# A fused attention and expert kernel: the first eleven stretches in another written order, and 1 / deviation of tiles 2 and 3 by GpSimd's power operation too

## The chip, the cores and the metric

The kernel runs on one core of a Trainium2 chip. The metric is device time in microseconds (us), the median of three runs. Five engines work side by side, each in the order of its own instruction list: TensorE (PE in the profile, its weight loads PEld), VectorE (DVE), ScalarE (ACT), GpSimd (POOL) and SyncE (SP), which here only issues transfers. ACT can issue transfers on a queue of its own.

## The reference

The input `x` is 2048 tokens of 640 values in bf16. It is normalized; the attention has 32 heads of 192 and, for all tokens, the last 512 keys and values of a cache. Its output is gated by an expert block that changes two tokens only.

```python
xn = _layernorm(x, axis=-1)                      # (x - mean) / sqrt(var + 1e-5)
q = (xn @ wq) -> heads;  k, v = last 512 rows of each head's cache
p = softmax(q @ k^T * 192 ** -0.5);  s = (p @ v) -> rows @ wo
r = xn @ w_r; the two tokens with the largest r get y = (silu(x_sel w_gate) * (x_sel w_up)) w_down * sigmoid(r)
g = silu(xn, with y added at those two tokens)
return x + s * g
```

## The kernel before

**Tiling.** The tokens are 16 tiles of 128 (n = 0 to 15), in four blocks of four tiles (t5). Heads are taken in pairs; two pairs make a group (g). A step i is one block with one pair: `steps[i]` is (g, t5, pr) with the pair innermost, so steps 0 and 1 are block 0 with pairs 0 and 1, steps 2 and 3 block 1, and so on to 8 steps for a group. A step has four units, one for each token tile, so unit n belongs to step n // 4. Units are worked in stretches: S.0 has units 0 and 1, S.1 units 2 and 3, S.2 units 4 to 6, then three in each stretch; 86 stretches in all. One stretch computes scores, row maxima, exponentials and their transposes for its units, and beside them the q projection of later steps (`q`), the product with v for the units of the stretch before (`O`) and the output projection (`W`).

**Order.** Nothing is scheduled by a planner: `manual_schedule` keeps every engine to the order in which the program calls it. For the first eleven stretches (S.0 to S.10) and what comes ahead of them this order is the token list `FIRST`, written out by hand; from S.11 on the function `stretch(j)` makes it, and a list `LAST` closes the kernel. Each token calls one function through `first(token)`. All engines read the same list; a token adds to the engine it names, so moving it past a token of another engine changes nothing, and moving it past one of the same engine, or the same queue, does.

**The tokens.** `x.t.lo.hi` loads token tiles of block t; `k.p.h`, `v.p`, `wq.p` load keys, values and q weights of pair p, `wo.g.pr` half of a group's output weights (SyncE's queue; with `.a`, ACT's). `kT.p` transposes the keys by DMA, `kt.q.e` half of pair 0's on TensorE. `bn.n.c` is one half of tile n's statistics on VectorE, the second half with the aggregate; `as.n` is both on ACT, in two passes. `sq` and `rc` make 1 / deviation by ACT's square root and VectorE's reciprocal; `pw.lo.hi` makes it on GpSimd, in four small operations of which the second is a power (line 212). `sx` and `ex` load ACT's tables for the square root and the exponential. `ap.n.e` applies the normalization, `turn.n.e` transposes a tile on TensorE with the copy on the engine named, `xT.lo.hi` transposes tiles by DMA. `q.i.c` is one third of step i's q (five matmuls; with `.lo.hi` for half a block), `qe.i.c.e` its eviction: the engine letter counts only without the trailing `.lo.hi`, with it ACT does it. `S.j` are the scores of a stretch in two passes (lines 315 and 322), `M` a row maximum (VectorE), `E` an exponential (ACT), `P.n` the DMA transpose of a unit's probabilities, `R` the reciprocal of the sums, `O.n` and `OO.n.m` the products with v, `Oe.n.e` their eviction, `T.j` the DMA transpose of a stretch's outputs, `W.w` the output projection of a token tile for one group, `We.w.e` its eviction. `B.j.s` runs background work of the expert block; for j up to 10 there is none, so these tokens do nothing.

**What holds an instruction back.** TensorE writes into eight banks: two of tag f (q, the transposes, single `O`) and six of tag p (scores, `OO`, `W`). A bank comes free with the eviction of what it held. SyncE issues its transfers one after the other, and each of eight semaphores is taken again only when the transfer before on it has landed. The block buffer of `x` has two slots, so block 2's load waits until block 0 has been applied.

Of the kernel before, what the change touches and what calls it, by code (L numbers as in the profile page):

```python
# [21 lines left out]
def kernel(ctx, tc, A_x, A_k_cache, A_v_cache, A_wq, A_wo, B_x, B_w_r, B_w_gate, B_w_up, B_w_down, out):  # L22
    nc = tc.nc
    P = 128
    _, S, D = A_x.shape
# [754 lines left out]
    for j in range(2, NST):  # L780
        due = sum(st_of[4 * i] <= j + 1 for i, _ in todo)
        k = max(due, 2) if j % 4 != 1 else max(due, 3)
# [3 lines left out]
        k = 2 if len(ready) >= 2 and len(q_in[j]) <= 2 and (done + 1) <= 1.5 * (j - 4) else 1  # L786
        k = {NST - 4: 1, NST - 3: 1, NST - 2: 3, NST - 1: 2}.get(j, k)
# [69 lines left out]

    for token in FIRST:
# [43 lines left out]
```

## Time and profile before

| | us |
|---|---|
| median of 3 runs | 809.0 |
| the runs | 807.45, 809.0, 809.56 |
| the profiled execution | 808.71 |
| its span | 806.9 |
| TensorE busy in the span | 785.0 (97%) |
| VectorE, ACT, GpSimd busy | 623.1, 480.5, 171.9 |

The span is what the profile covers; the rest of the execution's time lies around it. TensorE's busy time counts a matmul from its issue to a modelled end. In the views that follow, a timeline row gives the start in us, the duration, the engine, the source line, the operation, output and inputs, and in brackets how long the engine had been idle and what ended that. "SPq" is SyncE issuing a transfer; its duration is that of the issue. A row of transfers gives output and input, the number of issues, the size and the median time from issue to landing.

### The profile page before, as it was taken

To read this page: it belongs to the slowest core of one execution; us is meant where nothing else is said; L and a number is where in the kernel's file an instruction comes from. 1 tells how busy PE (TensorE), PEld (TensorE's weight loads), DVE (VectorE), ACT (ScalarE), POOL (GpSimd) and SP (SyncE) were. 2 spreads that over 40 slices of the span, in tenths; PEclk is the share of its full clock that TensorE was granted. 3 is DMA by queue.
4 is the path that set the end of the run, shared out by engine and by line. 5 is a ranking of instruction groups with operands and counts; after the bars stand their busy time and mean duration, and the time that the engine had idled before them with its cause. 6 is when DMAs were issued, how large, how long until landed. Compare 5 with 4: busy or idle time off the path is not lost. (4 is left out here: it accounts for less than half of the span.)

```text
span 806.9 us, 15632 instructions
## 1 busy us (share of the span) xinstructions
PE 785.0 (97%) x5748; PEld 481.6 (60%) x5748; DVE 623.1 (77%) x1242; ACT 480.5 (60%) x1299; POOL 171.9 (21%) x187
## 2 busy tenths in 40 slices
PE   7799999999999999999999999999999999999996
PEld 3355555666566665666656665666665666566665
DVE  6775478989887777777777777777788888777786
ACT  5796666565556655665555565566556865565560
POOL 0330000000000000000001899920000000265954
PEclk9999999999999999999999999999999999999999
DMA  8999898799979999799997899869997899997994
GB/s 224 201 209 219 159 208 134 134 187 183 187 124 206 198 210 210 128 209 213 188 229 145 163 180 202 160 122 184 201 166 134 148 180 209 167 194 153 167 177 117
DMA packets 453389, 143.80 MB, mean 178 GB/s; under 512 B 422350, under 2 KB 452816, under 8 KB 453312
## 3 DMA queue, kind: packets, MB, share of 16 engines
q1 hardware_dynamic: 451712, 139.94, 93.3%
q0 software_dynamic: 928, 2.50, 1.1%
q8 instruction: 45, 0.74, 0.4%
q10 hardware_dynamic: 672, 0.36, 0.1%
q14 instruction: 32, 0.26, 0.1%
HBM read 39.98 MB, written 2.62 MB: 53 GB/s over the span
## 5 line engine op out<-in xcount | busy, mean ns | idle before, releaser
L337 ACT ACTIVATE pexp<-sc,nm 128x512 bf16<-128x512 f32 x512 | 348.0, 695 | 287.4 <-issue 241.8
L330 DVE TENSOR_REDUCE nm<-sc 128x1 f32<-128x512 f32 x512 | 315.0, 681 | 74.8 <-PE sc L322 74.8
L301 PE MATMUL q_ps<-xnT,wq_p 128*128 128x512 bf16 (+1 forms) x975 | 227.4, 379 | 7.5 <-DMA xnT<-xn 2.6
L404 PE MATMUL w_ps<-wo_g,oT 128*128 128x320 bf16 x1542 | 223.6, 299 | 0.8 <-DMA wo_g<-in_A_wo_dram 0.6
L404 PEld LDWEIGHTS <-oT 128*128 128x128 bf16 x1542 | 150.1, 98 | 72.0 <-issue 1.5
L356 PE MATMUL o_ps<-v_sb,pT 128*128 128x192 bf16 x2048 | 185.2, 246 | 4.4 <-DMA pT<-pexp 4.4
L356 PEld LDWEIGHTS <-pT 128*128 128x128 bf16 x2048 | 171.1, 98 | 18.2 <-DMA pT<-pexp 5.3
L371 DVE TENSOR_TENSOR o_sb<-o_ps,lsum 128x384 bf16<-128x384 f32 x245 | 134.9, 556 | 49.2 <-PE o_ps L356 31.0
L301 PEld LDWEIGHTS <-wq_p 128*128 128x128 bf16 x975 | 89.0, 98 | 132.8 <-issue 41.3
L315 PE MATMUL sc<-kT,qT 128*128 128x512 bf16 x512 | 125.4, 379 | 0.5 <-DVE o_sb L371 0.3
L418 DVE TENSOR_TENSOR s_acc<-s_acc,w_ps 128x320 f32<-128x320 f32 x192 | 92.1, 483 | 32.1 <-PE w_ps L404 32.1
L337 ACT ACTIVATION_READ_ACCUMULATOR pexp<-sc,nm 128x1 f32 x512 | 109.6, 214 | 0.0
L293 ACT ACTIVATE qT<-q_ps 128x512 bf16<-128x512 f32 (+1 forms) x184 | 101.5, 605 | 3.4 <-PE q_ps L301 3.2
L315 PEld LDWEIGHTS <-qT 128*128 128x128 bf16 x512 | 48.9, 98 | 41.7 <-issue 0.7
L322 PE MATMUL sc<-kT,qT 64*128 64x512 bf16 x512 | 70.3, 380 | 0.0
L643 POOL TENSOR_TENSOR s_acc<-s_acc,xn 128x640 f32<-128x640 f32 x16 | 22.4, 1401 | 114.1 <-DVE s_acc L418 114.1
L322 PEld LDWEIGHTS <-qT 64*128 64x128 bf16 x512 | 18.0, 94 | 47.0 <-issue 36.2
L622 POOL TENSOR_TENSOR xn<-xn,yh 128x640 bf16<-128x640 bf16 x32 | 44.6, 1393 | 2.7
L612 POOL DMA_DIRECT2D y_d<-y_sb x4 | 2.2, 551 | 172.5 <-DVE y_sb L609 172.5
L644 POOL TENSOR_TENSOR s_acc<-s_acc,x_fin 128x640 f32<-128x640 f32 x16 | 22.4, 1398 | 62.8 <-DMA x_fin<-in_A_x_dram 61.9
L489 POOL DMA_DIRECT2D c_d<-cand x1 | 0.6, 551 | 158.6 <-DVE cand L487 158.6
L621 POOL TENSOR_SCALAR yh<-y_bc,oh 128x640 bf16<-128x640 bf16 x32 | 25.6, 798 | 4.5 <-DMA y_bc<-y_d 2.9
(104 smaller groups left out, 222.8 us busy)
## 6 DMA issues: line engine op xcount, KB each, us to landing
wq_p<-in_A_wq_dram SPq DMA_DIRECT2D x16, 480.0 KB, 5.3
wo_g<-in_A_wo_dram SPq DMA_DIRECT2D x16, 480.0 KB, 4.5
v_sb<-in_A_v_cache_dram SPq DMA_DIRECT2D x16, 384.0 KB, 3.9
k_raw<-in_A_k_cache_dram SPq DMA_DIRECT2D x31, 192.0 KB, 3.3
pT<-pexp SPq DMA_TRANSPOSE x256, 3.7
x_fin<-in_A_x_dram SPq DMA_DIRECT2D x16, 160.0 KB, 2.8
x_in<-in_A_x_dram SPq DMA_DIRECT2D x6, 320.0 KB, 4.1
wgu<-in_B_w_gate_dram SPq DMA_DIRECT2D x15, 128.0 KB, 2.6
```

The source lines that it names most:

```text
L293: nc.scalar.activation(out=out, in_=in_, func=ACT.Copy, scale=scale)
L301: nc.tensor.matmul(q_ps, lhsT=wq_of[g * PAIRS + pr][:, dc, c * P:(c + 1) * P], rhs=xnT[:, t5 * 4 + lo:t5 * 4 + hi, dc, :], start=(dc == 0) ...
L315: nc.tensor.matmul(sc_of[n][hh], lhsT=qT_of[i][:, 2 * hh, u * P:(u + 1) * P], rhs=kp[:, :, 2 * hh, :], start=True, stop=False)
L322: nc.tensor.matmul(sc_of[n][hh], lhsT=qT_of[i][hs, 1, u * P:(u + 1) * P], rhs=kp[hs, :, 1, :], start=False, stop=True)
L330: nc.vector.tensor_reduce(out=nm_of[j][:, c:c + 1], in_=sc_of[n][hh], axis=AX.X, op=ALU.max, negate=True)
L337: nc.scalar.activation(out=pe_of[n][:, hh, :], in_=sc_of[n][hh], func=ACT.Exp, bias=nm_of[j][:, c:c + 1], scale=1.0, accum_out=l_of[j][:, ...
L356: nc.tensor.matmul(ps[:, hh, :], lhsT=pT_of[n][:, hh, jj, :], rhs=v_sb[:, hh, jj, :], start=(jj == 0), stop=(jj == NJ - 1))
L371: nc.vector.tensor_tensor(out=osb_of[j][:, m], in0=ps, in1=l_of[j][:, 2 * m:2 * m + 2].unsqueeze(2).to_broadcast([P, 2, Dh]), op=ALU.mult)
L404: nc.tensor.matmul(w_ps, lhsT=oT_of[j][:, stretches[j].index(n), c % 3, :], rhs=wo_of[g][:, c, lo:hi], start=(c == 0), stop=(c == CPG - 1))
L418: nc.vector.tensor_tensor(out=acc, in0=acc, in1=w_ps, op=ALU.add)
L621: nc.gpsimd.tensor_scalar(out=yh, in0=M["y_bc"][:, j, :], scalar1=M["oh"][:, n, j:j + 1], scalar2=0.0, op0=ALU.mult, op1=ALU.add)
L622: nc.gpsimd.tensor_tensor(out=xn[:, n, :], in0=xn[:, n, :], in1=yh, op=ALU.add)
```

## The change

The tokens of the prologue and of S.0 to S.10 are put into another order, and some change their engine. Ahead of S.0, tile 0 is now loaded from ACT's queue and tile 2 from SyncE's; wq.0 goes ahead of tile 3; half of pair 0's keys, half of pair 1's and wq.1 are issued by ACT. The second half of pair 0's keys and the copy of tile 1 are taken from the transposing bank by VectorE, that of tile 0 by ACT. `sq.2.4` and `rc.2.4` are replaced by `pw.2.4`. The exponential's table is loaded ahead of the first q evictions. In the first eleven stretches the statistics of tiles 4, 8, 12 and 15 go from VectorE to ACT, and those of 9 and 13 from ACT to VectorE. `kT.1` moves from S.0 to S.1, behind the loads of block 2 and `v.0`; `v.1` goes ahead of `v.0`. `P.1` moves from S.0 to S.1, behind them too; `turn.2`'s copy goes from ACT to VectorE. O.0 moves from S.2 to S.1. In S.6 to S.8, `P.15` goes between the two transposes of tiles 12 to 15; `v.2` goes from S.6 to S.7, `wq.2` from SyncE in S.6 to ACT in S.7, `k.3.0` from S.8 to S.7; `P.19`, `P.20` and `P.21` stand together in S.8, ahead of `k.3.1` and `wq.3`. The matmuls are the same; W.4, W.5 and others change their place by a few tokens. From S.11 on nothing is changed. Seven lines of each side of the diff follow: the prologue, S.0 to S.2 and S.6 to S.8.

```diff
-x.0.2.3.a x.0.0.1 x.0.1.2 bn.0.0 bn.1.0 bn.0.1 bn.1.1 sq.0.1 sq.1.2 rc.0.1 k.0.0 rc.1.2 k.0.1 ap.0.v ap.1.v x.0.3.4 sx wq.0 kt.0.a x.1.0.2 kt.1.a turn.0.v turn.1.a x.1.2.4 q.0.0.0.2 q.0.2.0.2 B.2.0 bn.2.0 qe.0.0.v.0.2 q.0.1.0.2 qe.0.2.v.0.2 bn.3.0 qe.0.1.v.0.2 bn.2.1 wq.1 bn.3.1 sq.2.4 bn.7.0 ex rc.2.4 ap.3.v k.1.0 ap.2.v
- S.0 turn.3.a M.0.1 M.0.0 turn.2.a E.0.0 q.0.0.2.4 bn.7.1 q.0.2.2.4 k.1.1 M.1.0 qe.0.0.v.2.4 M.1.1 E.1.0 v.0 q.0.1.2.4 bn.6.0 kT.1 bn.6.1 qe.0.2.a.2.4 qe.0.1.v.2.4 as.5 bn.4.0 x.2.0.2 v.1 bn.4.1 E.1.1 E.0.1 P.1
- S.1 M.2.0 E.2.0 M.2.1 q.1.2 x.2.2.4 pw.4.8 E.2.1 qe.1.2.a bn.8.0 bn.8.1 P.2 q.1.0 M.3.0 M.3.1 qe.1.0.a ap.7.g ap.5.v q.1.1 B.3.3 ap.4.v E.3.0 ap.6.v E.3.1 P.0 xT.4.6 qe.1.1.a
- S.2 R.0 M.4.0 M.5.0 bn.11.0 O.1 as.9 O.0 M.4.1 bn.11.1 E.4.0 as.10 xT.6.8 M.5.1 M.6.0 pw.8.12 Oe.0.a E.4.1 E.5.0 Oe.1.a E.6.0 R.1 P.3 q.2.0 M.6.1 qe.2.0.v q.2.1 x.3.2.4 q.2.2 B.4.0 B.2.1 qe.2.1.v B.2.3 P.4 ap.11.v T.0 E.6.1 P.6 O.2 E.5.1 qe.2.2.v
...
- S.6 Oe.12.a M.17.0 ap.13.g xT.14.16 q.5.2 xT.12.14 M.16.0 M.18.0 M.17.1 v.2 E.17.0 P.15 B.8.0 E.16.0 qe.5.2.v M.16.1 wo.1.0 E.18.0 E.16.1 R.5 B.7.0 k.2.0.a B.5.2 W.2 M.18.1 E.18.1 q.6.0 E.17.1 B.8.3 B.5.0 qe.6.0.a B.4.2 k.2.1 W.1 We.1.v OO.13.14 Oe.13.v We.2.a wq.2 Oe.14.v P.16 O.15
- S.7 M.19.0 P.17 M.20.0 M.21.0 Oe.15.a E.19.0 M.19.1 M.21.1 B.6.0 T.4 q.6.1 P.18 R.6 E.20.0 T.5 M.20.1 qe.6.1.a q.6.2 E.19.1 W.3 E.20.1 qe.6.2.v E.21.0 OO.16.17 Oe.16.a E.21.1 We.3.a O.18 Oe.17.v W.4 P.19 We.4.a P.21
- S.8 Oe.18.v B.9.1 M.22.0 E.22.0 k.3.0 M.23.0 wq.3 R.7 q.7.0 q.7.1 M.22.1 M.24.0 E.23.0 k.3.1 P.20 M.23.1 E.22.1 M.24.1 E.23.1 E.24.0 E.24.1 qe.7.1.v W.6 OO.19.20 P.22 W.5 We.5.a We.6.a qe.7.0.a Oe.19.v O.21 Oe.20.v
...
+B.3.3 x.0.0.1.a x.0.1.2 k.0.0 bn.0.0 k.0.1.a bn.1.0 x.0.2.3 bn.0.1 sx sq.0.1 wq.0 bn.1.1 sq.1.2 kt.0.a rc.0.1 ap.0.v rc.1.2 kt.1.v x.0.3.4 ap.1.v bn.2.0 turn.0.a turn.1.v q.0.0.0.2 q.0.2.0.2 ex bn.2.1 qe.0.0.v.0.2 k.1.0.a bn.3.0 bn.3.1 qe.0.2.v.0.2 wq.1.a x.1.2.4 q.0.1.0.2 qe.0.1.a.0.2 x.1.0.2 pw.2.4
+S.0 k.1.1 as.4 ap.2.v ap.3.v turn.2.v turn.3.a M.0.0 q.0.0.2.4 E.0.0 M.1.0 q.0.2.2.4 qe.0.0.v.2.4 E.1.0 bn.7.0 q.0.1.2.4 M.0.1 qe.0.2.v.2.4 v.1 qe.0.1.a.2.4 bn.6.0 B.2.0 bn.7.1 E.0.1
+S.1 bn.6.1 x.2.0.2 M.1.1 q.1.2 x.2.2.4 as.5 q.1.0 pw.4.8 v.0 M.2.1 E.1.1 qe.1.2.a M.2.0 E.2.0 R.0 M.3.1 E.2.1 as.8 q.1.1 ap.6.g ap.4.v ap.5.v M.3.0 B.3.2 E.3.0 qe.1.0.v P.0 kT.1 bn.11.0 B.3.1 bn.9.0 ap.7.v O.0 qe.1.1.v E.3.1 bn.11.1 P.1
+S.2 B.3.0 P.2 B.2.1 bn.9.1 xT.4.6 xT.6.8 M.4.0 as.10 P.3 B.4.0 M.5.0 pw.8.12 Oe.0.a M.4.1 O.1 E.5.0 M.5.1 q.2.0 E.5.1 x.3.0.2 Oe.1.v E.4.0 M.6.0 E.6.0 qe.2.0.v T.0 x.3.2.4 E.4.1 P.4 q.2.1 R.1 q.2.2 M.6.1 qe.2.1.v B.2.2 ap.8.g qe.2.2.v E.6.1 ap.9.g O.2
...
+S.6 q.5.1 M.16.0 E.16.0 B.4.1 xT.14.16 B.8.0 B.5.0 P.15 ap.13.g M.17.1 M.16.1 M.17.0 qe.5.1.a B.7.3 xT.12.14 E.16.1 k.2.0 q.5.2 M.18.0 B.4.2 M.18.1 W.2 R.5 E.17.0 wo.1.0 E.18.0 We.2.v E.17.1 k.2.1 B.7.1 P.16 OO.13.14 E.18.1 W.1 q.6.0 B.6.2 qe.5.2.v P.18 Oe.13.a Oe.14.a We.1.v O.15 T.4 P.17
+S.7 Oe.15.v qe.6.0.v M.20.0 q.6.1 B.10.3 M.19.0 M.21.0 qe.6.1.v E.19.0 B.5.1 M.21.1 M.20.1 M.19.1 E.20.0 q.6.2 E.21.0 E.19.1 E.20.1 W.3 O.18 W.4 T.5 wq.2.a v.2 qe.6.2.v E.21.1 We.4.v OO.16.17 k.3.0 R.6 We.3.a Oe.16.v Oe.17.a
+S.8 M.22.0 Oe.18.a M.23.1 E.22.0 B.9.1 P.21 M.22.1 q.7.0 R.7 M.24.1 P.19 M.23.0 P.20 E.22.1 E.23.0 B.7.0 q.7.1 qe.7.0.a k.3.1 qe.7.1.a E.23.1 W.6 M.24.0 W.5 We.6.v E.24.0 wq.3 E.24.1 OO.19.20 B.6.0 P.22 Oe.19.a T.6 We.5.v Oe.20.a B.9.0
...
```

More of the change, by code (lines that the diff above doesn't have):

```diff
@@ new lines @@
+S.2 B.3.0 P.2 B.2.1 bn.9.1 xT.4.6 xT.6.8 M.4.0 as.10 P.3 B.4.0 M.5.0 pw.8.12 Oe.0.a M.4.1 O.1 E.5.0 M.5.1 q.2.0 E.5.1 x.3.0.2 Oe.1.v E.4.0 M.6.0 E.6.0 qe.2.0.v T.0 x.3.2.4 E.4.1 P.4 q.2.1 R.1 q.2.2 M.6.1 qe.2.1.v B.2.2 ap.8.g qe.2.2.v E.6.1 ap.9.g O.2
+S.3 Oe.2.a ap.11.v M.7.0 P.5 M.8.0 M.8.1 as.12 ap.10.g O.3 E.7.0 Oe.3.a P.6 E.8.0 q.3.1 q.3.0 M.9.1 M.9.0 E.8.1 M.7.1 bn.13.0 E.7.1 qe.3.0.v OO.4.5 xT.8.10 R.2 E.9.0 Oe.4.v E.9.1 xT.10.12 qe.3.1.a Oe.5.v q.3.2 qe.3.2.v bn.13.1 P.8
+S.4 T.1 O.6 as.15 B.2.3 q.4.1 B.7.2 P.7 Oe.6.a M.10.1 P.9 R.3 M.10.0 E.10.0 M.12.0 q.4.0 E.12.0 wo.0.0 M.11.0 wo.0.1 E.10.1 E.11.0 P.10 qe.4.1.v T.2 M.12.1 OO.7.8 M.11.1 E.12.1 qe.4.0.v E.11.1 O.9 Oe.7.v Oe.8.v Oe.9.v as.14
@@ new lines @@
+S.5 pw.12.16 P.11 q.4.2 M.13.0 E.13.0 M.13.1 P.12 M.14.0 M.14.1 M.15.0 E.14.0 ap.15.g B.5.3 B.4.3 E.14.1 q.5.0 qe.5.0.a E.13.1 M.15.1 qe.4.2.v W.0 B.6.3 ap.14.v E.15.0 OO.10.11 R.4 Oe.10.a E.15.1 T.3 B.5.2 Oe.11.a P.14 O.12 Oe.12.a ap.12.g P.13 We.0.v B.6.1
+S.6 q.5.1 M.16.0 E.16.0 B.4.1 xT.14.16 B.8.0 B.5.0 P.15 ap.13.g M.17.1 M.16.1 M.17.0 qe.5.1.a B.7.3 xT.12.14 E.16.1 k.2.0 q.5.2 M.18.0 B.4.2 M.18.1 W.2 R.5 E.17.0 wo.1.0 E.18.0 We.2.v E.17.1 k.2.1 B.7.1 P.16 OO.13.14 E.18.1 W.1 q.6.0 B.6.2 qe.5.2.v P.18 Oe.13.a Oe.14.a We.1.v O.15 T.4 P.17
@@ new lines @@
+S.7 Oe.15.v qe.6.0.v M.20.0 q.6.1 B.10.3 M.19.0 M.21.0 qe.6.1.v E.19.0 B.5.1 M.21.1 M.20.1 M.19.1 E.20.0 q.6.2 E.21.0 E.19.1 E.20.1 W.3 O.18 W.4 T.5 wq.2.a v.2 qe.6.2.v E.21.1 We.4.v OO.16.17 k.3.0 R.6 We.3.a Oe.16.v Oe.17.a
+S.8 M.22.0 Oe.18.a M.23.1 E.22.0 B.9.1 P.21 M.22.1 q.7.0 R.7 M.24.1 P.19 M.23.0 P.20 E.22.1 E.23.0 B.7.0 q.7.1 qe.7.0.a k.3.1 qe.7.1.a E.23.1 W.6 M.24.0 W.5 We.6.v E.24.0 wq.3 E.24.1 OO.19.20 B.6.0 P.22 Oe.19.a T.6 We.5.v Oe.20.a B.9.0
+S.9 P.23 M.26.0 kT.3 B.10.1 M.26.1 O.21 Oe.21.v M.25.1 E.26.0 q.8.0 M.25.0 E.26.1 E.25.0 E.25.1 W.7 q.7.2 B.10.2 M.27.0 qe.8.0.a P.24 OO.22.23 E.27.0 M.27.1 qe.7.2.v E.27.1 T.7 P.26 R.8 B.8.1 Oe.22.v Oe.23.a q.8.1 P.25 kT.2 We.7.v
@@ L856 @@
+S.10 M.28.0 M.28.1 M.29.0 qe.8.1.a O.24 R.9 B.8.3 B.8.2 B.9.2 Oe.24.v P.27 E.28.0 v.3 M.30.0 E.28.1 q.9.0 qe.9.0.v E.29.0 M.30.1 E.30.0 OO.25.26 M.29.1 B.10.0 P.28 Oe.25.a q.8.2 E.29.1 B.9.3 E.30.1 O.27 qe.8.2.a Oe.26.a T.8 W.9 P.29 P.30 Oe.27.a W.8 wo.1.1 We.9.a T.9 We.8.a
     """.split()
```

5 lines of the change are left out of this document (removed).

## The prediction

> **What bounds the kernel now.** I read the page's first part, then busy time by windows whose edges are the starts of the score matmuls of chosen stretches, then TensorE's waits in the first 112 us, then the timelines of TensorE and of the DMA queue there.
>
> ```profile
> span 806.9 us, 15632 instructions
> PE 785.0 (97%) x5748; PEld 481.6 (60%) x5748; DVE 623.1 (77%) x1242; ACT 480.5 (60%) x1299; POOL 171.9 (21%) x187
> ```
>
> TensorE sets the time: 21.9 us of idle are all that any order can win. The windows (stretch, its length, then busy time of PE, PEld, DVE, ACT and POOL, PE's granted clock, DMA share, GB/s) say where it is idle before the ordinary stretches take over; S.3 begins at 35.31, S.6 at 60.01, S.7 at 71.86, S.8 at 81.69, S.9 at 93.00, S.11 at 111.66.
>
> ```profile
> 16.38:35.31 18.93, 14.52 (x90) 7.32 (x89) 14.75 (x34) 17.86 (x50) 6.43 (x14) 1.00 0.96 202
> 35.31:60.01 24.70, 23.91 (x171) 13.80 (x170) 19.57 (x40) 20.18 (x56) 6.64 (x19) 1.00 1.12 212
> 60.01:71.86 11.85, 9.97 (x72) 5.87 (x71) 6.67 (x13) 6.51 (x19) 0.00 (x0) 1.00 1.16 204
> 71.86:81.69 9.83, 9.82 (x74) 5.98 (x72) 5.46 (x10) 7.04 (x20) 0.00 (x0) 1.00 1.13 230
> 81.69:93.00 11.31, 9.72 (x72) 5.96 (x70) 5.46 (x10) 5.54 (x16) 0.00 (x0) 1.00 1.09 199
> 93.00:111.66 18.66, 18.66 (x136) 11.36 (x135) 11.43 (x22) 13.67 (x38) 0.00 (x0) 1.00 0.86 153
> ```
>
> Idle is length less the first number: 4.41 us up to S.3, 0.79 in S.3 to S.5, 1.88 in S.6, 0.01 in S.7, 1.59 in S.8, none after. That is 8.7 us within reach of the new order, and the stretches from S.11 on are untouched. The waits name the releasers:
>
> ```profile
> PE o_ps L356 <- DMA pT<-pexp: 3.6, 3, 1.7
> PE q_ps L301 <- DMA xnT<-xn: 2.6, 1, 2.6
> PE q_ps L301 <- DMA wq_p<-in_A_wq_dram: 1.8, 1, 1.8
> PE q_ps L301 <- ACT xnT L259: 1.2, 1, 1.2
> ```
>
> and TensorE's timeline their places:
>
> ```profile
> 9.66 3.38 PE L301 MATMUL q_ps<-xnT,wq_p 128*128 128x256 bf16 x15 [1.77 <-DMA wq_p<-in_A_wq_dram]
> ...
> 16.38 1.88 PE L301 MATMUL q_ps<-xnT,wq_p 128*128 128x256 bf16 x15 [1.19 <-ACT xnT L259]
> ...
> 26.07 0.82 PE L322 MATMUL sc<-kT,qT 64*128 64x512 bf16 x6
> ...
> 31.40 3.41 PE L301 MATMUL q_ps<-xnT,wq_p 128*128 128x512 bf16 x15 [2.55 <-DMA xnT<-xn]
> ...
> 71.19 0.83 PE L356 MATMUL o_ps<-v_sb,pT 128*128 128x192 bf16 x8 [1.69 <-DMA pT<-pexp]
> ...
> 90.04 0.83 PE L356 MATMUL o_ps<-v_sb,pT 128*128 128x192 bf16 x8 [1.59 <-DMA pT<-pexp]
> ```
>
> The two late waits (O.15 at the end of S.6, O.20 in S.8) are waits for transposes that stood behind loads in SyncE's queue:
>
> ```profile
> 63.03 0.81 SPq L124 DMA_DIRECT2D v_sb<-in_A_v_cache_dram  x1
> 63.95 3.59 SPq L342 DMA_TRANSPOSE pT<-pexp  x1
> ...
> 83.80 3.49 SPq L342 DMA_TRANSPOSE pT<-pexp  x1
> ```
>
> P.15, issued right after the v load, held the queue 3.59 us. P.20, behind two k loads and a wq load, held it 3.49.
>
> **The start, to the second half of the first q.** No matmul is added or removed, so only waits count. Rows of single operations (the number after the comma is the mean in ns):
>
> ```profile
> L337 ACT ACTIVATE pexp<-sc,nm 128x512 bf16<-128x512 f32 x62 | 42.2, 692 | 11.2 <-DVE nm L330 8.8 <-issue 1.1 <-DMA pT<-pexp 0.8
> L330 DVE TENSOR_REDUCE nm<-sc 128x1 f32<-128x512 f32 x62 | 39.1, 676 | 15.9 <-PE sc L322 15.9
> ...
> L163 DVE BATCH_NORM_STATS2 stats<-x_in 128x6 f32<-128x320 bf16 x22 | 10.0, 477 | 3.4 <-DMA x_in<-in_A_x_dram 3.4
> ...
> L291 DVE TENSOR_SCALAR qT<-q_ps 128x512 bf16<-128x512 f32 x11 | 7.5, 678 | 3.1 <-PE q_ps L301 3.1
> ...
> L251 DVE TENSOR_SCALAR xn<-x_in,mv,rstd 128x640 bf16<-128x640 bf16 x10 | 4.4, 472 | 0.0
> L234 ACT ACTIVATE junk_a<-x_in,nmr 128x640 bf16<-128x640 bf16 x5 | 4.1, 828 | 0.2
> ...
> L212 POOL TENSOR_TENSOR rstd<-rstd,half_m 128x4 f32<-128x4 f32 x3 | 3.1, 1023 | 0.2
> ...
> L259 ACT COPY xnT<-tp 128x640 bf16<-128x640 bf16 x3 | 2.0, 693 | 0.0
> ...
> L211 POOL TENSOR_SCALAR rstd<-mv 128x4 f32<-128x4 f32 x3 | 0.6, 197 | 2.3 <-ACT junk_a L234 2.3
> ```
>
> and one window's row with two of ACT's timeline:
>
> ```profile
> 8.00:10.00 2.00, 0.34 (x2) 0.28 (x3) 1.93 (x7) 1.13 (x2) 0.00 (x0) 0.89 1.04 361
> ...
> 13.08 0.38 ACT L293 ACTIVATE qT<-q_ps 128x256 bf16<-128x256 f32 x1 [0.68 <-PE q_ps L301]
> ...
> 13.66 1.28 ACT L241 ACT_TABLE_LOAD   x1
> ```
>
> The wq load now goes ahead of token tile 3 (160 KB). At the 361 GB/s of that window this is 0.45 us or a little more: the first q starts near 9.1 instead of 9.66, its third eviction ends near 12.9 instead of 13.46, and S.0, whose second pass follows that eviction, near 13.9. Tile 3 lands later for it, near 9.6. Two half statistics (0.48 each) end at 10.8 with their aggregate, GpSimd's first step and power (0.20 + 1.02) at 12.1, two applies on VectorE (0.47 each) at 13.0, still under S.0. The power on two columns is not in the trace; between 0.20 (a plain step) and 1.02 (four columns) I take 1.02, and either is hidden. Without that cover the chain would cost what it overhangs, nothing before 0.9 us. The exponential's table load (1.28) moves from ahead of the two copies to under the first q, and the square root of tiles 2 and 3 vanishes. But as.4 (two passes over tile 4, the second kind 0.83) now stands ahead of ACT's copy: it runs from 12.9 to 14.6, the copy (0.69) to 15.3. The second half of q starts there instead of 16.38: a lead of 1.0.
>
> **S.1 and S.2 take it back.** From turn.2.v (14.2) to qe.1.1.v VectorE has a copy (about 0.5), 8 row maxima (5.4), 6 half statistics with their aggregates (3.3), a reciprocal (0.2), 3 applies (1.4) and 2 evictions that ACT had (1.4): 12.2 us, so 26.4. The second score pass of S.2 needs that last eviction; it began at 26.07 before. The lead is gone there, whatever ACT does.
>
> Then q.2.0 waits for xT.6.8. Its way through SyncE's queue:
>
> ```profile
> 14.40 1.55 SPq L119 DMA_TRANSPOSE kT<-k_raw  x1
> ...
> 23.09 2.64 SPq L342 DMA_TRANSPOSE pT<-pexp  x2
> ...
> 25.82 3.18 SPq L262 DMA_TRANSPOSE xnT<-xn  x2
> ```
>
> Before, kT.1 went early. Now x.2.0.2, x.2.2.4 and v.0 come first, the first of them waiting for the landing of wq.1, which ACT issues near 11.8, between its evictions. I put that landing at 16.5 (the load has to share with k, v and k) and the three issues by 18.4. P.0 can go at 18.6: after the copy at 15.3 ACT has three exponentials (0.69) and three evictions (0.38). If it is held as P.15 was, it goes out by 22.2, kT.1 by 23.8, P.1 and P.2 by 26.4, and the two xT start 0.6 later than 25.82. If nothing is held, the last xT waits only for ap.7.v, and its issue ends 1.0 sooner than before. Nearer the middle, I take 0.2 us of gain at S.3, between -0.6 and +1.0. O.0 moves ahead of S.2; its 0.8 us is only shifted.
>
> **S.3 to S.5** have the same PE work less one q, which S.6 gets. VectorE and ACT lose and gain statistics and evictions of about a microsecond each way per stretch, beside TensorE's 23.91. The idle of 0.79 stays: gain 0, bounds -0.8 and +0.8.
>
> **S.6.** P.15 now goes between xT.14.16 and xT.12.14, and v.2 moves to S.7. It is needed at the end of a stretch of 9.97 us of TensorE work: the 1.69 goes, and the rest of S.6's 1.88 with it. xT.12.14 is one transpose later than before, and q.6.0 follows it; I give back 0.3. Gain 1.6. The loads k.2.0, wo.1.0, k.2.1 now stand ahead of P.16, which is needed only at the end of S.7.
>
> **S.7 and S.8.** P.21, P.19 and P.20 go out together, ahead of k.3.1 and wq.3, but behind v.2 and k.3.0, and beside wq.2 on ACT's queue. P.21 can go about 0.5 before S.8 begins, after the last exponential of S.7. O.20 was due 6.8 us into S.8 (90.04 - 1.59 - 81.69) and now has a W more ahead of it, over 8 us. At 1.3 for each issue the three are out in 4. The bounds are 0 and 1.59; since wq.2 shares the engines, I take 1.2.
>
> **Sum.** 0.2 + 0 + 1.6 + 1.2 = 3.0 us. The profiled execution took 808.71 (span 806.9 and 1.8 around it) and gives 805.7; the median of the runs lies 0.3 higher, so 806.0.
>
> **Rivals.**
>
> *Transposes behind loads, at the new places (slower).* If each transpose queued behind loads costs what P.15 did, and wq.1 lands as late as it did before, the order loses.
>
> ```profile
> wq_p<-in_A_wq_dram SPq DMA_DIRECT2D x1, 480.0 KB, 7.8
> ...
> pT<-pexp SPq DMA_TRANSPOSE x1, 7.2
> ```
>
> wq.1 issued at 11.8 lands at 19.6, the three loads are out by 21.5, P.0 at 25.1, kT.1 26.6, P.1 and P.2 29.3, the xT pair 32.5; TensorE went on 2.4 us after the pair's issue (29.00 to 31.40), so q.2.0 starts near 34.9: 3.5 lost. In S.8, P.21 held 3.59, P.19 1.3 and P.20 landing 7.2 later make 11.6 us into S.8 against 8.4: 3.2 of wait in place of 1.6. With S.6's 1.6 won, 3.5 + 1.6 - 1.6 = 3.5: 812.5, or about 811 with one of the two. It decides from a landing of wq.1 later than about 17.5. For it: both rows. Against: 7.8 was measured behind two 320 KB loads in the same queue, and wq.1 is now on another. Chance 0.24.
>
> *The DMA engines are the second bound (no change).* Shares of 1.12, 1.16, 1.13 and 1.09 from 35.31 to 93.00 are 64.9 us of DMA work; at the highest, 1.16, they need 55.9 of the 57.7 us. Then at most 1.8 is saved and the waits reappear under other names: 807.2. Against: S.9 and S.10 run at 0.86, so work can slip there. Chance 0.16.
>
> *The clock falls a second time.*
>
> ```profile
> 10.00:12.00 2.00, 2.00 (x12) 1.38 (x10) 0.66 (x2) 0.38 (x1) 0.00 (x0) 0.50 1.18 303
> 25.00:30.00 5.00, 3.49 (x28) 1.72 (x25) 3.48 (x8) 4.93 (x14) 0.44 (x3) 1.00 1.17 209
> ```
>
> The granted clock was 0.50 when the first half q ran, 3.38 us against 1.88 for the same 15 matmuls at 16.38; it was 1.00 around the 2.55 us wait. My S.2 leaves over 3 us idle ahead of q.2.0. A second such spell costs 1.5: 807.5. Chance 0.06. [...]
>
> *Everything hides (faster).* The lead of 1.0 survives and S.3 to S.8 lose all their idle of 4.3: 803.7; with the first q at full clock 1.5 less, 802.2. Against: VectorE's 12.2 us. Chance 0.14.
>
> **How the numbers follow.** The forecast has 0.40 and a range of its own of 804.5 to 807.3 from the bounds above. What this measurement can tell from no change is 0.3%, 2.4 us: 806.6 to 811.4. Faster: 0.14 and 0.31 of the forecast, 0.45. Same: 0.09 of it, 0.16 and 0.06, 0.31. Slower: 0.24. Leaving out the far ends of the first and last rival, some 0.2, the range is 802.5 to 812.0.
>
> **What would show it.** Right: second half of q near 15.3 with ACT's copy as releaser; the second score pass of S.2 within 0.5 of 26.07, released by VectorE; S.3 at 34.3 to 35.9; no wait over 0.5 for pT at the end of S.6; S.9 and S.11 some 3 us sooner (S.9 has one O more than before). Wrong: S.2 released by DMA kT near 29, an SP transpose held over 3 us in S.7 or S.8 with TensorE behind it, or idle in S.3 to S.5 well over 0.79.

## The result, and the profile after

Over 17 runs of each kernel the changed one takes 803.38 us (800.23 to 806.74), the kernel before 807.9 (804.88 to 809.67): a ratio of 0.9947, 95% interval 0.9935 to 0.996, or 4.5 us less. The forecast was 806.0 with 802.5 to 812.0. The profiled execution took 803.23, its span 801.5.

The page's first part for the changed kernel:

```profile
span 801.5 us, 15649 instructions
PE 785.5 (98%) x5748; PEld 481.5 (60%) x5748; DVE 625.2 (78%) x1243; ACT 482.0 (60%) x1303; POOL 174.8 (22%) x194
```

The busy time of TensorE is nearly the same (785.0 before), so the difference is idle time. Its windows, with the edges again at the starts of the score matmuls of S.3, S.6, S.7, S.8, S.9 and S.11 (columns as before):

```profile
33.43:57.69 24.26, 22.96 (x165) 13.12 (x164) 19.93 (x39) 20.88 (x57) 7.63 (x21) 1.00 1.09 208
57.69:68.88 11.19, 10.81 (x78) 6.43 (x77) 6.21 (x12) 7.47 (x23) 0.07 (x1) 1.00 1.12 199
68.88:78.43 9.55, 9.55 (x72) 6.02 (x71) 7.55 (x14) 4.88 (x14) 0.00 (x0) 1.00 1.10 213
78.43:87.32 8.89, 8.89 (x64) 5.36 (x63) 5.73 (x12) 6.76 (x19) 0.00 (x0) 1.00 1.21 233
87.32:107.15 19.83, 19.68 (x144) 11.86 (x142) 11.09 (x21) 14.66 (x42) 0.00 (x0) 1.00 1.00 185
```

Length less busy time gives the idle per stage, and the edges give the lead. One execution of each kernel is compared here; how far these numbers move from one execution to the next is shown with the experiments.

| | before | after | gain | forecast |
|---|---|---|---|---|
| start of S.3 | 35.31 | 33.43 | 1.88 | 0.2 |
| idle in S.3 to S.5 | 0.79 | 1.30 | -0.51 | 0 |
| idle in S.6 | 1.88 | 0.38 | 1.50 | 1.6 |
| idle in S.7 | 0.01 | 0.00 | 0.01 | 0 |
| idle in S.8 | 1.59 | 0.00 | 1.59 | 1.2 |
| idle in S.9 and S.10 | 0.00 | 0.15 | -0.15 | 0 |

The sum is 4.3; S.11 begins at 107.15 instead of 111.66, and 0.9 more comes after it, where nothing was changed. S.6 now holds one third of a q that stood in S.5 (78 matmuls against 72), and S.9 holds O.21, so busy times of these stages are not compared, idle is.

TensorE's timeline at the places that the prediction named:

```profile
9.41 1.89 PE L301 MATMUL q_ps<-xnT,wq_p 128*128 128x256 bf16 x15 [0.67 <-DVE xnT L259]
...
14.14 1.91 PE L301 MATMUL q_ps<-xnT,wq_p 128*128 128x256 bf16 x15 [0.78 <-ACT xnT L259]
...
22.33 0.82 PE L356 MATMUL o_ps<-v_sb,pT 128*128 128x192 bf16 x8 [1.03 <-DVE qT L291]
24.06 2.68 PE L315 MATMUL sc<-kT,qT 128*128 128x512 bf16 x6 [0.91 <-DMA kT<-k_raw]
26.68 1.23 PE L322 MATMUL sc<-kT,qT 64*128 64x512 bf16 x6
...
29.48 3.40 PE L301 MATMUL q_ps<-xnT,wq_p 128*128 128x512 bf16 x15 [0.80 <-ACT pexp L337]
...
67.13 1.25 PE L301 MATMUL q_ps<-xnT,wq_p 128*128 128x512 bf16 x5 [0.38 <-DMA xnT<-xn]
68.22 0.82 PE L356 MATMUL o_ps<-v_sb,pT 128*128 128x192 bf16 x8
```

The first q ran at full clock in this execution (1.89 us where the profile before has 3.38), and the second half starts 2.24 sooner. S.2's six score matmuls took 2.68 where the same six take 1.46 elsewhere: the half-clock spell is still there, but it has moved to S.2 (granted clock 0.53 from 24 to 26 and 0.61 from 26 to 28). O.15 at 68.22 has no wait in front of it. The DMA queue's timeline has the new places of the transposes:

```profile
12.87 0.88 SPq L100 DMA_DIRECT2D x_in<-in_A_x_dram  x2
...
17.21 1.37 SPq L342 DMA_TRANSPOSE pT<-pexp  x1
18.69 1.52 SPq L119 DMA_TRANSPOSE kT<-k_raw  x1
20.30 3.39 SPq L342 DMA_TRANSPOSE pT<-pexp  x2
23.78 3.06 SPq L262 DMA_TRANSPOSE xnT<-xn  x2
...
61.00 1.74 SPq L342 DMA_TRANSPOSE pT<-pexp  x1
62.83 2.18 SPq L262 DMA_TRANSPOSE xnT<-xn  x1
...
77.36 5.44 SPq L342 DMA_TRANSPOSE pT<-pexp  x3
```

P.0 is not held (1.37), the pair of xT goes out at 23.78 instead of 25.82, P.15 takes 1.74 instead of 3.59. P.20, which before went out at 83.80, is now the last of three that begin at 77.36, 1.1 us ahead of S.8, and are out at 82.80.

### The profile page after: what moved, and what is told of

Read it like the earlier page. It is cut to its first block, busy times and chain, and to the rows that moved or that the text cites. A ratio compares the mean times of both kernels' runs of the same rounds, so it can differ in the third digit from the quotient of the medians.

```text
span 801.5 us, 15649 instructions
## 1 busy us (share of the span) xinstructions
PE 785.5 (98%) x5748; PEld 481.5 (60%) x5748; DVE 625.2 (78%) x1243; ACT 482.0 (60%) x1303; POOL 174.8 (22%) x194
## 3 DMA queue, kind: packets, MB, share of 16 engines
HBM read 39.98 MB, written 2.62 MB: 53 GB/s over the span
## 5 line engine op out<-in xcount | busy, mean ns | idle before, releaser
L371 DVE TENSOR_TENSOR o_sb<-o_ps,lsum 128x384 bf16<-128x384 f32 x239 | 131.6, 557 | 40.2 <-PE o_ps L356 22.0
L293 ACT ACTIVATE qT<-q_ps 128x512 bf16<-128x512 f32 (+1 forms) x179 | 98.8, 606 | 1.3 <-PE q_ps L301 1.1
```

The source lines that it names most:

```text
L293: nc.scalar.activation(out=out, in_=in_, func=ACT.Copy, scale=scale)
L371: nc.vector.tensor_tensor(out=osb_of[j][:, m], in0=ps, in1=l_of[j][:, 2 * m:2 * m + 2].unsqueeze(2).to_broadcast([P, 2, Dh]), op=ALU.mult)
```

## The experiments

Every experiment was compared with the kernel before on the same chip. Edits are shown as pieces of the token list.

**Which half of the order carries the gain.** The first two kernels divide the list at S.3. One has the new prologue to S.2 and the old rest, with the five tokens mended that would otherwise be done twice or not at all:

```diff
 O.3
-ap.8.g
+ap.11.v
 Oe.2.v M.7.0
-x.3.0.2
+P.6
 B.3.1
-ap.9.v
 M.9.0
```

> The changed order up to S.2, the old order from S.3 on (with ap.11.v and P.6 in S.3 in place of what the new S.2 already does: ap.8, ap.9, x.3.0.2). Theory A (the gain has two independent parts, a start that is 1.9 us sooner at S.3 and two late waits for transposes that are worth about 3): S.3 begins near 33.4, the waits of O.15 and O.20 come back with 1.6 us each, and the kernel is 1.5 to 2.3 us faster than before. Rival B (the start's lead carries the rest with it, the late waits go because everything is earlier): 4 us or more faster. Rival C (the lead is eaten by the late waits, which hang on SyncE's queue alone): within 0.7 us of before.

Measured: 806.48, ratio 0.9975 (0.9958 to 0.9991), 2.1 us faster as theory A says. Its profiled execution fits less well: S.3 began at 34.51 and not near 33.4, and O.15 waited 0.81, O.20 1.55. The other has the old list to S.2 and the new one from S.3:

```diff
 Oe.2.a
-ap.11.v
+x.3.0.2 ap.8.g ap.9.g
 M.7.0
...
 Oe.3.a
-P.6
 E.8.0
```

> The old order up to S.2, the changed one from S.3 on (ap.8.g, ap.9.g and x.3.0.2 in S.3 in place of ap.11.v and P.6, which the old S.2 has). Theory A: S.3 begins near 35.3 as before, no wait over 0.5 us for O.15 and O.20, 0.7 us more idle in S.3 to S.5, and the kernel is 2 to 3 us faster than before. Rival B (all hangs on the start): within 0.7 us of before. Together with the run of the start alone the two gains should add to the 4.5 us of the whole change.

Measured: 805.49, ratio 0.9961 (0.9947 to 0.9975). The parts give -2.1 and -3.1 us, their sum -5.2, against -4.5 (-5.3 to -3.2) for the whole: they add within their intervals, and the start's part, which I had at 0.2, is real. The profiled execution of the second one, the slowest of its twelve, missed its forecast in one place: S.3 began at 38.91 and not near 35.3, since q.2.0 waited 2.92 and then took 6.21 in place of 3.41. O.15 and O.20 did not wait. The stretch starts say the same: S.3 to S.9 takes 57.69 us in the kernel before and 58.34 with the new start alone, but 53.41 with the new rest alone and 53.89 in the whole change. (0.67 of the last two is O.21, which moved behind S.9's start.)

**Is it only the two turns?** In the kernel before, P.15 goes ahead of xT.12.14, v.2 to S.7, P.20 ahead of the loads of pair 3:

```diff
 q.5.2
+P.15
 xT.12.14 M.16.0 M.18.0 M.17.1
-v.2
 E.17.0
-P.15
...
 P.21
+v.2
...
+P.20
 k.3.0 M.23.0 wq.3 R.7 q.7.0 q.7.1 M.22.1 M.24.0 E.23.0 k.3.1
-P.20
```

> The kernel before with four tokens moved: P.15 ahead of xT.12.14, v.2 from S.6 to S.7, and P.20 ahead of k.3.0, wq.3 and k.3.1. If the place of a transpose among the loads in SyncE's queue is the cause of the two late waits, both go and the kernel is 2.5 to 3.4 us faster than before. Rival (the DMA engines are the bound, so a wait that is removed comes back under another name): less than 1 us faster, with new waits for transposes in S.7 to S.9.

Measured: 809.55, ratio 1.0008 (0.999 to 1.0025). No gain: the theory in this bare form is wrong. TensorE's timeline of that run, in S.6 and S.8:

```profile
69.19 1.69 PE L301 MATMUL q_ps<-xnT,wq_p 128*128 128x512 bf16 x5 [2.97 <-DMA xnT<-xn]
70.67 3.08 PE L404 MATMUL w_ps<-wo_g,oT 128*128 128x320 bf16 x12
...
92.20 0.83 PE L356 MATMUL o_ps<-v_sb,pT 128*128 128x192 bf16 x8 [0.31 <-DMA pT<-pexp]
```

O.15's wait is gone, but q.6.0, which in the old order stands well ahead of it, now waits 2.97 for the transpose that was pushed back, and the matmuls behind it ran at half clock (0.50 from 70 to 72; W 3.08 against 1.79). In S.8 the same run did gain: O.20 waits 0.31 instead of 1.59, and the stretch takes 10.04 instead of 11.31. So in the old order the turn in S.6 does not help while q.6.0 stands where it did; the change moves q.6.0 back too. The next kernel adds that:

```diff
-q.6.0
 E.17.1 B.8.3 B.5.0
-qe.6.0.a
...
 P.16
+q.6.0
 O.15
...
 Oe.15.a
+qe.6.0.a
```

> The kernel before with the moves of the earlier run (P.15 ahead of xT.12.14, v.2 to S.7, P.20 ahead of k.3.0, wq.3 and k.3.1) and, beside them, q.6.0 moved behind W.1 and OO.13.14, ahead of O.15, with its eviction behind O.15's. If that run gained nothing because q.6.0 then waited 2.97 us for the transpose that had been put back by one place, and TensorE was at half clock behind that wait, the wait for xT.12.14 is under 0.7 us now and the kernel is 2 to 3.3 us faster than before. Rival (the DMA engines are the bound): it stays within 1 us of before, and waits for transposes of 2 us or more show in S.6 to S.9.

Measured: 806.21, ratio 0.997 (0.995 to 0.999), -2.6 us. In its timeline neither q.6.0 nor O.15 waits:

```profile
70.47 1.24 PE L301 MATMUL q_ps<-xnT,wq_p 128*128 128x512 bf16 x5
71.55 0.82 PE L356 MATMUL o_ps<-v_sb,pT 128*128 128x192 bf16 x8
```

Four moves out of the long list (P.15, v.2, P.20, and q.6.0 with its eviction) thus give most of what the rest of the new order gave (-3.1). The opposite test takes the turn out of the changed kernel and leaves q.6.0 where the change put it:

```diff
-P.15
 ap.13.g M.17.1 M.16.1 M.17.0 qe.5.1.a B.7.3 xT.12.14
+v.2 P.15
...
 wq.2.a
-v.2
```

> The changed kernel with P.15 behind xT.12.14 again and v.2 in S.6 again. Theory (the turn of the pexp tile late behind the xT transpose sets O.15's start): a wait of 1.5 to 3 us returns at the end of S.6 and the time is 1.5 to 3 us longer than the changed kernel's. Rival (q.6.0, which stands behind, has the slack): no wait over 0.8 us there and within 0.8 us of the changed kernel.

Measured: 804.63, ratio 0.9959 (0.9939 to 0.9979). Its S.6 shows one short wait:

```profile
69.19 0.83 PE L356 MATMUL o_ps<-v_sb,pT 128*128 128x192 bf16 x8 [0.81 <-DMA pT<-pexp]
```

S.6 is 11.61 long instead of 11.19, 0.4 lost where the theory said 1.5 to 3. The time is 1.0 us above the changed kernel's by the ratios and 1.3 by the medians, between the theory and the rival (within 0.8), and the intervals overlap. The queue's timeline:

```profile
63.78 1.34 SPq L124 DMA_DIRECT2D v_sb<-in_A_v_cache_dram  x1
65.23 1.24 SPq L342 DMA_TRANSPOSE pT<-pexp  x1
```

Right behind the same v load, P.15 is not held here (1.24, against 3.59 before). Nor is it in every execution of the old order. These are the profiled executions that have the whole old or the whole new order from S.3 on (the kernels not met so far follow below):

| us | old order: before, start alone, warm start, warm kernel before | new order: changed (two), rest alone, square root, wq.1 on SyncE, warm changed (two) |
|---|---|---|
| P.15's issue | 3.59, 2.79, 1.23, 1.23 | 1.74, 1.37, 1.51, 2.34, 1.51, 1.50, 1.46 |
| idle in S.3 to S.5 | 0.79, 1.74, 0.97, 1.14 | 1.30, 0.00, 0.73, 0.45, 0.42, 0.19, 0.27 |
| idle in S.6 | 1.88, 1.41, 1.85, 1.46 | 0.38, 0.39, 0.83, 0.95, 0.55, 0.69, 0.93 |
| idle in S.8 | 1.59, 1.55, 0.76, 0.44 | 0.00, 0.00, 0.00, 0.00, 0.04, 1.27, 0.71 |

With issues of 1.23, behind the same v load, S.6 was idle as long as with 3.59: O.15 then had no wait of its own, but q.6.0 had one for xT.12.14. The warm start shows it:

```profile
67.34 1.25 PE L304 MATMUL q_ps<-xnT,wq_p 128*128 128x512 bf16 x5 [1.65 <-DMA xnT<-xn]
```

And the length of the issue is not what O.15 waited for. P.15's transpose landed at 71.15 in the kernel before and with the start alone (issues of 3.59 and 2.79) and at 71.50 in the warm start (1.23). So the 3.59 that the prediction rests on belongs to that execution, and what sets the landing was not tried and stays open. One move that the list of changes does not name is near it: k.2.0 was issued from ACT's queue at 65.76, while P.15 was being issued, and now goes from SyncE's behind both transposes of tiles 12 to 15. With P.15's turn taken out, the idle of S.6 (0.81) lies within what the new order has with it (0.38 to 0.95): a gain of the turn in the new order is not shown. S.6 as a whole gained in every one of these executions; in the old order the two moves of P.15 and q.6.0 together do it, and what else moved may have part in it.

**Is it the clock?** The profile before shows the first q at half clock, that of the changed kernel does not. The kernel before, with seven matmuls on zeros (128x512, into the bank of the warm-up) right ahead of the first q:

> The kernel before with seven matmuls of 512 columns on zeros ahead of the first q, in the wait for wq. If the half clock of the first q (3.38 us against 1.88) comes from TensorE's idleness ahead of it, its 15 matmuls take 1.9 us, and the second half of q starts 1.0 to 1.5 us sooner than 16.38; what is left of that at S.3 is open, between 0 and 1.5 us, as ACT is busy throughout. Rival (the clock falls whatever is issued in that wait, or falls later instead): the spell at half clock stays or shows up elsewhere, and nothing is gained.

Measured: 806.87, ratio 0.9982 (0.9963 to 1.0). The first q took 1.90 and its second half began at 15.12, but a spell then fell on q.2.0 (5.16 instead of 3.41, at a granted clock of 0.68 from 30 to 32 and 0.50 from 32 to 34). That q had waited 2.36 us for its data, and S.3 began at 35.55. The interval reaches from no gain to 3 us, so this run alone settles nothing. A second sample of the changed kernel shows that the spell has no fixed place:

> The changed kernel again, on the same chip as the others of this call. Its ratio to before is 0.9935 to 0.996. If the place of the half-clock spell is a matter of chance, this execution has it in another place or at another length than the first, which had it in S.2 (24 to 28 us) and none in the first q.

Measured: 803.32, ratio 0.9947 (0.9926 to 0.9968). Its timeline:

```profile
9.00 3.31 PE L301 MATMUL q_ps<-xnT,wq_p 128*128 128x256 bf16 x15 [0.68 <-DVE xnT L259]
...
15.31 1.91 PE L301 MATMUL q_ps<-xnT,wq_p 128*128 128x256 bf16 x15 [0.78 <-ACT xnT L259]
...
25.23 1.46 PE L315 MATMUL sc<-kT,qT 128*128 128x512 bf16 x6 [0.92 <-DMA kT<-k_raw]
...
30.57 3.40 PE L301 MATMUL q_ps<-xnT,wq_p 128*128 128x512 bf16 x15 [2.36 <-DMA xnT<-xn]
```

The spell is in the first q (granted clock 0.50 from 10 to 12) and not in S.2 (1.00 from 24 to 28); S.3 starts at 34.50, 1.07 later than in the first sample, and the span is still 799.8. And its windows for S.3 to S.5 and S.6:

```profile
34.50:56.99 22.49, 22.49 (x166) 13.34 (x164) 19.47 (x39) 20.64 (x57) 6.44 (x13) 1.00 1.09 214
56.99:68.19 11.20, 10.81 (x78) 6.42 (x76) 6.22 (x12) 7.60 (x23) 1.30 (x9) 1.00 1.09 192
```

No idle in S.3 to S.5: the 1.30 of the first profile belongs to that execution, not to the order. S.6 agrees to 0.01.

The strongest test keeps both kernels warm. In the changed one, matmuls on zeros fill the waits (3 of 512 ahead of turn.1, 6 of 256 ahead of each half of the first q, 4 of 512 ahead of O.0, of S.2 and of q.2.0); in the kernel before, 7, 8 (of 256), 6 and 10 stand ahead of the first q, its second half, q.1.1 and q.2.0.

> The changed kernel with matmuls on zeros in TensorE's waits of the start: 3 of 512 columns ahead of turn.1, 6 of 256 each ahead of the two halves of the first q, 4 of 512 ahead of O.0, of S.2 and of q.2.0, written to banks that the next group clears. The products that count are the same. Theory (TensorE's clock halves after a thinly filled stretch, once or twice among the first 35 us, and each spell costs about 1.6 us): no window up to 36 us is granted less than 0.95, and it is 1 to 2 us faster than the changed kernel. Rival (the fillers only stand in the way, the spells are not tied to idleness): a spell still shows, and it is 0 to 2 us slower than the changed kernel.

Measured: 801.79, ratio 0.9917 (0.9895 to 0.9939). The same kernel a second time, and the warm kernel before on the same chip:

> The changed kernel with matmuls on zeros in its early waits, a second sample beside the kernel before with such matmuls. Theory: 801 to 802.5, a ratio of 0.990 to 0.994 to before. If the first sample was a lucky chip: 803 or more.

> The kernel before, with matmuls on zeros in its early waits (7 x 512 ahead of the first q, 8 x 256 ahead of its second half, 6 x 512 ahead of the second pass, 10 x 512 ahead of q.2.0), so that TensorE's granted clock does not fall. If the change's gain lies in its order (theory), this is 2 to 3 us faster than before and stays 3.5 to 4.5 us slower than the changed kernel with such matmuls. If the gain was only the clock (rival), it comes within 1.5 us of that one.

Measured: 802.82, ratio 0.9938 (0.9919 to 0.9958), and 809.37, ratio 1.001 (0.9993 to 1.0027). TensorE's timeline of the warm kernel before:

```profile
10.87 1.89 PE L312 MATMUL q_ps<-xnT,wq_p 128*128 128x256 bf16 x15
...
31.29 3.52 PE L312 MATMUL q_ps<-xnT,wq_p 128*128 128x512 bf16 x15
```

Its first q is 1.5 us shorter but starts 1.2 later behind the fillers, and q.2.0 starts at 31.29 against 31.40: where it waited 2.55 before, the fillers stand; its S.3 begins at 35.30 (35.31 before). The 2 to 3 us that I expected of warmth here did not come. The granted clock was 1.00 in every 2 us window from 8 to 38 of both warm kernels. The mean granted clock over the runs was 0.998 in all three samples. With equal clocks the changed order is 6.6 us ahead by the medians (809.37 - 802.82), more than the 3.5 to 4.5 that I had expected: the rival that the gain was the clock is refuted. How much of the 6.6 the fillers themselves cost the kernel before is not separated. S.3 begins at 32.79 and 32.12 in the warm changed kernel, so the start's lead is there at full clock too (2.5 and 3.2 us). The warm changed kernel is the fastest version; its two samples lie 0.6 and 1.6 below the changed kernel's, but their intervals overlap with it.

**The power in place of the square root.** In the changed kernel, tiles 2 and 3 of the first block get their 1 / deviation by ACT and VectorE again, and so the exponential's table is loaded after it:

```diff
 q.0.2.0.2
-ex
 bn.2.1
...
 x.1.0.2
-pw.2.4
+sq.2.4 ex rc.2.4
```

> The changed kernel with 1 / deviation of tiles 2 and 3 again by ACT's square root and VectorE's reciprocal, the exponential's table loaded behind it (sq.2.4, ex and rc.2.4 in the place of pw.2.4). If the power operation is worth what it takes off ACT's path to the second half of the first q (0.29 + 1.28 us, then as.4 and the copy behind them), that half starts 1.3 to 1.8 us later than in the changed kernel, and the kernel is 0.7 to 1.8 us slower than it. Rival (VectorE's list from there to S.2 is the bound, so the power operation is worth nothing): within 0.5 us of the changed kernel.

Measured: 807.14, ratio 0.9981 (0.9966 to 0.9995), some 2.7 us above the 0.9947 of the changed kernel (0.34% of 807.9), and 3.8 by the medians on the same chip. I had expected 0.7 to 1.8. TensorE's timeline, then ACT's:

```profile
15.73 2.40 PE L301 MATMUL q_ps<-xnT,wq_p 128*128 128x256 bf16 x15 [2.26 <-ACT xnT L259]
...
32.02 3.40 PE L301 MATMUL q_ps<-xnT,wq_p 128*128 128x512 bf16 x15 [3.04 <-DMA xnT<-xn]
```

```profile
11.63 0.29 ACT L223 ACTIVATE rstd<-mv,eps_t 128x2 f32<-128x2 f32 x1
11.93 1.28 ACT L241 ACT_TABLE_LOAD   x1
...
15.01 0.67 ACT L259 COPY xnT<-tp 128x640 bf16<-128x640 bf16 x1
```

The square root and the table load stand ahead of the copy that the second half of q needs: 15.01 instead of 13.40 in the changed kernel, and 1.59 us later starts that half. The table load took 1.28, as in the kernel before, and the next ACT instruction starts at 13.23, 0.02 after its end. At q.2.0 the loss is 2.5 us (32.02 against 29.48); the half-clock spell, which here falls on the second half of the first q (2.40 instead of 1.91) and S.1 (granted clock 0.73, 0.50 and 0.91 in the windows from 16 to 22), has part in it, as it has in the changed kernel's S.2. It is more than the whole new start gained by itself (2.1). The run puts back both the square root and the later table load and does not separate the two.

**Which queue loads wq.1.** My slower rival hung on its landing. Here k.1.0 and wq.1 are issued by SyncE again, in the changed kernel:

```diff
-k.1.0.a
...
-wq.1.a
...
 x.1.0.2
+k.1.0 wq.1
```

> The changed kernel with k.1.0 and wq.1 issued from SyncE's queue, right behind x.1.0.2, as in no version so far. Theory (x.2.0.2 goes when the softmax's last tile of the first block is written, whatever loads wq.1): within 1 us of the changed kernel. Rival (wq.1 queued later on SyncE and its transposes behind it late): over 1.5 us slower, with a wait of TensorE at the second pass or at q.2.0.

Measured: 804.16, ratio 0.9956 (0.994 to 0.9972): within 1 us of the changed kernel. Its queue:

```profile
12.77 0.89 SPq L100 DMA_DIRECT2D x_in<-in_A_x_dram  x2
```

The loads of x go out at 12.77 here and at 12.87 in the changed kernel: the queue of wq.1 does not matter to them.

## Why the prediction was right, point by point

The time lies inside the stated range, and the change is faster by more than the 0.3% that this measurement can tell. But 803.38 lies below the forecast's own range of 804.5 to 807.3; the nearest recorded time is the 803.7 of "Everything hides", which had a chance of 0.14. The kernel before, too, came out 1.1 lower over 17 runs than in the three on record, so gains compare better: 3.0 forecast, 4.5 measured. The largest miss is the start.

**The second half of the first q: lead 1.0 forecast, 2.24 measured.** The releaser was right (ACT's copy), its time was not. Rows of ACT and GpSimd of the changed kernel:

```profile
11.28 0.73 POOL L212 TENSOR_TENSOR rstd<-rstd,half_m 128x2 f32<-128x2 f32 x1
...
12.56 0.83 ACT L234 ACTIVATE junk_a<-x_in,nmr 128x640 bf16<-128x640 bf16 x1
...
13.40 0.69 ACT L259 COPY xnT<-tp 128x640 bf16<-128x640 bf16 x1
```

as.4 ended at 13.4, not 14.6, since the first q ended at 11.3 (9.41 + 1.89), where I had 12.5 from a start at 9.1 and the 3.38 at half clock. So the term that was off is the clock of the first q, which the prediction had put at half and named only under "Everything hides". In the second sample, whose first q was at half clock, the half started at 15.31, to 0.01 as forecast; with the start alone it was 15.39. The power on two columns took 0.73, less than the 1.02 that I took from four.

**"S.1 and S.2 take it back": wrong.** This is the step that failed. VectorE's timeline has the first and the last instruction of the list that I had put at 12.2 us:

```profile
13.12 0.49 DVE L259 COPY xnT<-tp 128x640 bf16<-128x640 bf16 x1 [0.28 <-PE tp L258]
...
23.42 0.67 DVE L291 TENSOR_SCALAR qT<-q_ps 128x512 bf16<-128x512 f32 x1
```

It ran 11.0 us from 13.12 and ended at 24.09, not at 26.4; my sum had added durations that overlap in the trace (two half statistics in a row take 0.88, not twice 0.48). The second score pass came at 26.68, 0.61 later than before and just outside the 0.5 that I had set, but the half clock put it there and no eviction. In the second sample S.2's first pass, too, was released by DMA kT, at 25.23, and the second pass came at 26.62 at full clock. That both lie near the forecast 26.4 is luck: another releaser put them there. kT as releaser is what I had listed as a sign of being wrong, but it cost 0.9 and not 4.

**The way to q.2.0: gain 0.2 forecast, 1.88 measured in the first sample,** outside my bounds of -0.6 and +1.0, and 0.81 in the second, inside them. I had x.2.0.2 wait for the landing of wq.1, at 16.5. It was issued at 12.87, and with wq.1 on the other queue at 12.77: the wait that I built into this chain did not exist. P.0 was not held. It went at 17.21 in the first sample, and the pair of xT at 23.78. The queue of the second sample has

```profile
18.38 1.37 SPq L342 DMA_TRANSPOSE pT<-pexp  x1
...
24.95 3.00 SPq L262 DMA_TRANSPOSE xnT<-xn  x2
```

P.0 is near the 18.6 of the forecast, since that also followed from ACT's exponentials and evictions, and the pair's issue ends at 27.95, 1.05 sooner than before (29.00): my case "nothing is held" to 0.05. What failed is that I took a gain between that case and the held one, which did not come, and reckoned with the first q at half clock only. In the five profiled executions with the new start and neither fillers nor the square root, S.3 begins at 33.43 and 33.22 with the first q at full clock and at 34.50, 34.51 and 34.83 with it at half clock. The old start in its four without fillers has 35.31, 36.78, 37.00 and 38.91; the first of these is the one that I forecast from, and in the other three q.2.0 took 6.10 to 6.21 at half clock. So a lead taken from one pair of executions is no measure; the start alone measured 2.1 over its runs.

**S.3 to S.5: nothing** was forecast; -0.51 in one execution, and no idle at all in the other. Over the executions of the table above the idle is 0.79 to 1.74 in the old order and 0.00 to 1.30 in the new one, so it leans to a gain and not to none.

**S.6: 1.6 forecast, 1.50 measured.** The size was right in this pair of executions (1.41 to 1.88 of idle before, 0.38 to 0.95 after, over the table), the mechanism only in part, so there is luck in it. P.15 ahead of xT.12.14, with the turn in S.8, gains nothing (ratio 1.0008); it needs q.6.0 behind W.1 and OO.13.14. And the long issue of P.15 was not the cause of the wait. I had given back 0.3 for q.6.0 without seeing that its place in the list decides between 0.38 and 2.97.

**S.8: 1.2 forecast, 1.59 measured.** The wait for P.20 went whole; in other executions of the old order it was 0.44 to 1.55. The transposes together took 5.44, not the 4 that I had put, but started early enough.

**The rivals.** Transposes behind loads at the new places: none was held ahead of q.2.0, and the one in S.8 was covered. DMA engines as a second bound: their share rose to 1.21 in S.8, over the 1.16 that I took for the highest, with no idle, and S.3 to S.9 took 53.89 us where this rival needs 55.9; refuted. Everything hides: nearly so, S.3 to S.8 kept 1.68 of their 4.27 us of idle in one execution.

**A second fall of the clock** came, but not at q.2.0, where the rival had put it: it fell on S.2. In the profiled changed kernel it stood in place of the spell of the first q; with the start alone and with P.15's turn taken out, which have the same start, both came (first q 3.22 and 2.97 for 1.89, S.2's scores 2.33 and 2.43 for 1.46). These windows of the changed kernel show the spell of S.2:

```profile
22.00:24.00 2.00, 0.82 (x8) 0.67 (x8) 2.00 (x5) 1.97 (x6) 1.07 (x2) 1.00 1.21 83
24.00:26.00 2.00, 1.94 (x5) 0.70 (x5) 1.27 (x5) 1.97 (x7) 0.19 (x1) 0.53 1.27 278
26.00:28.00 2.00, 2.00 (x10) 0.45 (x9) 0.68 (x2) 0.64 (x3) 1.60 (x4) 0.61 1.11 178
```

No single wait there was over 1.03; eight short matmuls (0.82 us) stood between two waits. I had gone by the length of single waits, and my 0.06 rested on that: no run shows a length from which the clock falls. The two samples, which have the same instructions, had their spells on S.2 and on the first q.

## What to carry to other kernels

When a transpose is moved ahead of another in one queue, look up the first reader of the one that was pushed back and move that too: without q.6.0 the two turns gained nothing, with it 2.6 us. Put table loads under a matmul and not ahead of a copy that the next matmul needs; here one table load and a tiny square root, 1.57 us together, cost some 2.7. Before a releaser goes into a sum, look for the wait itself: the one that I inferred for x.2.0.2 was not there. And take several profiles before a stage is priced: the wait of S.8 was 0.44 to 1.59 us, and the issue of P.15 1.23 to 3.59, in executions of one order.

## What the runs showed of the hardware

In the windows of these profiles a half-clock spell of TensorE lasted 3.4 us (ten spells) or 6.8 (three). In windows of 2 us the time at half clock is twice the sum of (1 - granted clock) times 2 us: 3.4 for the three windows above. With the two turns alone, where q.2.0 waits for data and then runs at half clock (6.15 us instead of 3.41), it is 6.8:

```profile
28.00:30.00 2.00, 0.00 (x0) 0.00 (x0) 1.31 (x4) 2.00 (x7) 1.62 (x5) 0.73 1.15 191
30.00:32.00 2.00, 1.87 (x5) 0.74 (x6) 0.00 (x0) 2.00 (x7) 1.72 (x2) 0.50 0.91 198
32.00:34.00 2.00, 2.00 (x6) 0.68 (x5) 0.69 (x1) 0.53 (x2) 0.00 (x0) 0.50 1.26 249
34.00:36.00 2.00, 2.00 (x7) 0.78 (x6) 1.04 (x2) 0.00 (x0) 0.00 (x0) 0.57 1.03 181
```

A spell falls in the first 40 us of every profiled execution without fillers but one (that with wq.1 on SyncE's queue): on the first q, on its second half and S.1, on S.2's scores or on q.2.0, in three of them in two of these places (the rest alone shows its first one by durations only: the first q took 3.37 at a recorded clock of 1.00). Two executions of the same instructions differ. The length of a wait alone does not decide. With the two turns alone another spell, of 3.4, followed a wait of 2.97 us, up to 69.19. At q.2.0 a spell came with waits of 2.36 (warm start) and of 2.62, 2.66 and 2.92, and none with waits of 2.36 (second sample), 2.47, 2.55 and 3.04.

Over the 17 runs of the changed kernel the mean granted clock lies between 0.991 (806.74 us) and 0.999 (800.23 us), and a line through them falls 0.6 us for each 0.001 and accounts for half of the variance. In the nine runs of the second sample it falls 0.3 and accounts for 7%, and the eight runs of the warm changed kernel, all at 0.998 or more, still spread from 801.43 to 804.37. So the clock explains a part of the spread between executions, and the rest is open. With the waits filled by matmuls on zeros the clock was 1.00 in every 2 us window from 8 to 38 of all three warm profiles. In the kernel before, whose q.2.0 waits 2.55 us for data without them, that gained nothing (1.001).

A transpose's issue time depends on more than the order of the queue: P.15 behind the same v load took 3.59, 2.79, 1.23 and 1.23 us in four executions with the same order from S.3 on. When the data is there is another matter: the transpose landed 3.6 us after the end of the issue of 3.59 and 4.6 after that of the warm start's 1.23.
